# A new priority table for the first part of an attention and softplus-FFN kernel, and one transpose for the last keys of two tiles

## The chip, the cores and the metric

The kernel runs on one core of a Trainium2 chip. TensorE (PE in the profile, with PEld for its weight loads), VectorE (DVE), ScalarE (ACT), GpSimd (POOL) and SyncE (SP, which issues all the DMAs of this kernel) run side by side, each through its own instructions in their order, and wait for one another through semaphores. The metric is the device time of one execution in microseconds, as the median of several executions. Smaller is better.

## The reference

Keys and values are averaged over groups of 8 positions, attention runs over the 72 pooled positions, and the result goes through a two-layer network with softplus between.

```python
batch, n_heads, seq, head_dim = (8, 8, 576, 64)     # q, k, v
k_p = k.reshape(B, H, Sp, pool, D).mean(axis=3)      # pool = 8, Sp = 72
v_p = v.reshape(B, H, Sp, pool, D).mean(axis=3)
scores = scale * np.matmul(q, k_p.transpose(0, 1, 3, 2))
scores = scores - np.max(scores, axis=-1, keepdims=True)
attn = np.exp(scores)
attn = attn / (np.sum(attn, axis=-1, keepdims=True) + 1e-09)
attn_out = np.matmul(attn, v_p)
x = attn_out.transpose(0, 2, 1, 3).reshape(B * S, H * D)     # 4608 x 512
h = x @ w_in                                                 # 512 x 2048
g = np.maximum(h, 0.0) + np.log1p(np.exp(-np.abs(h)))
out = g @ w_out                                              # 2048 x 512
```

## The kernel before

The 4608 tokens are cut into 18 chunks of 256, each of two tiles of 128 tokens. A chunk goes through attention (`qTp`: transposes of q; `sc`: scores; `E`: exponentials; `pm` and `pe`: probabilities; `ptp` and `ltp`: their transposes; `avp`: products with the pooled values; `x`: the result, split into a high and a low part) and then through the network (`h`: first product; `g`: softplus; `acc` or `m`: second product). The network has 16 blocks f of 128 hidden units. Every product with a weight is made of three: high by high, low by high, high by low. So each block of w_in and w_out has to be rearranged and split first: SP loads it (`stage` for blocks 0 to 10, `wst` for blocks 11 to 15), DVE makes five passes over it (`bits`, `clamp`, `shift`, `sign`, `lowest`), ACT rounds it (`high`) and DVE subtracts (`rest`). The fourth pass (`sign`) of blocks 11 to 15 waits for block 10, since their results lie where `stage` was.

Of the 72 pooled keys of a head the first 64 are called main (`pm`, transposed in `PT` as `ptp`) and the last 8 are called the ends (`pe`, transposed as `ltp`). In `av_products` the ends need three copies of their probabilities in the partitions of `lt_`: high, low and high again, R = 32 rows each, for two halves of the heads.

The program has two parts. The first holds the pooling of batches 0 and 1 (`batch`), the conversion of all weight blocks (`weights`), the attention of chunks 0 to 3 (`attend`) and the network of chunks 0 to 2 (`feed`). The second part, from chunk 3 on, repeats one pattern until the end. In each part all operations are first written down as objects with an engine, a cost in microseconds, what they come after and the slots (PSUM banks, buffers) that they hold; `Order.run` then makes a schedule of them, engine by engine. Among operations that could start, it takes the one with the highest `rank` (the longest path of costs behind it) plus `first`. The table `HASTE` adds a number to `first` of single operations by their place in the list, for the first part alone. So costs and table set the order in which each engine, SP's queue included, gets its instructions, and which of several buffers they take. At run time each engine keeps to this order, and waits where something isn't there yet.

The names for what follows: `kvl` holds the last 64 positions of k and v of a batch, `kvst` half of its other keys or values, `kvlp` and `kps` are their pooling products on PE, `vps` the one for values, `kT` the transposed pooled keys. The exponentials of chunks 0 to 2 are made head by head from PSUM (`exp_sum`), those of chunk 3 at once (`exponential`); both need a table on ACT other than softplus does.

Of the kernel before, what the change touches and what calls it, by code (L numbers as in the profile page):

```python
# [9 lines left out]
F32 = mybir.dt.float32  # L10
# [98 lines left out]
def pooled_attention_softplus_ffn(  # L109
# [269 lines left out]
    class Tile:  # L379
# [47 lines left out]
        def exp_sum(self, j, ps, tag):  # L427
            if j == 0:
                self.sm = small.tile([P, H], F32, tag="sm" + tag, name="sm")
            for m in range(HP):  # L430
                h = 4 * (m // 2) + 2 * j + m % 2
                nc.scalar.activation(out=e_[self.c][:, self.t, h], in_=self.view(ps)[:, m],  # L432
                                     func=AF.Exp, scale=-1.0, bias=self.mn[:, j, m:m + 1],
                                     accum_out=self.sm[:, h:h + 1])
# [37 lines left out]
        def PT_out(self, ps):  # L472
            if self.c not in pt_:
                pt_[self.c] = one.tile([P, HP, CT], F32, tag="Z", name="pT")
            nc.scalar.copy(out=pt_[self.c][:, :, self.ts],
                           in_=ps.rearrange("p (m i) -> p m i", m=HP))

        def last(self, ps):
            for a in range(2):
                nc.tensor.transpose(out=ps[0:3 * R, a * P:(a + 1) * P],  # L480
                                    in_=self.pe[:, a].rearrange("p n k -> p (n k)"), identity=ident)

        def last_high(self, ps):

            if self.c not in last_:
                last_[self.c] = one.tile([3 * R, 2, CT], F32R, tag="Y", name="lt_")
            nc.scalar.copy(out=last_[self.c][:, :, self.ts],
                           in_=ps[0:3 * R, 0:2 * P].rearrange("p (a i) -> p a i", a=2))

        def last_low(self, ps):  # L490
            o = last_[self.c][R:2 * R, :, self.ts]
            nc.vector.tensor_tensor(
                out=o, in0=ps[R:2 * R, 0:2 * P].rearrange("p (a i) -> p a i", a=2),
                in1=o.bitcast(F32), op=ALU.subtract)

# [375 lines left out]
    def act(n):  # L871
        return 0.14 + 0.00094 * n
# [10 lines left out]
    def weights(f):  # L883
# [5 lines left out]
        def load(i):  # L889
            def fn():  # L890
                if early:
                    if not i:
                        x["raw"] = stage_at(f % NS)
                    st = x["raw"][:, 1 - i]
                else:
                    st = x["raw", i] = one.tile([P, 4 * 2 * P], I32, tag=stages[i].name, name="wst")
                if i:
                    nc.sync.dma_start(out=st, in_=wo32[f * P:(f + 1) * P, :])
                else:
                    for r in range(2):  # L900
# [85 lines left out]
    def batch(b):  # L986
# [23 lines left out]
        o_left = op(SYNC, 1.3, load_left, slots=[ld], lag=2.2)  # L1010
        o_k = [op(SYNC, 1.5, load(k, i), slots=[st[i]], lag=2.2) for i in range(2)]
        o_v = [op(SYNC, 1.5, load(v, i), slots=[vt[i] or vt[0]], lag=2.2) for i in range(2)]

# [21 lines left out]

        o = op(PE, 1.0, left_products, [o_left], [ld, s_left])
        o_kl = op(DVE, dve2(512), left_keys, [o], [s_left, s_kp])
# [7 lines left out]
        for i in range(2):  # L1045
# [10 lines left out]
            def products(i=i, N=N):  # L1056
                ps = bank(s_k, "kps").rearrange("p (h d) -> p h d", h=H)
                for r in range(N):
                    nc.tensor.matmul(out=ps[0:KM, HP * i:HP * (i + 1)], lhsT=zm,  # L1059
                                     rhs=x["k", i][:, :, r], start=r == 0, stop=r == N - 1)  # L1060
            halves.append(op(PE, 0.1 + 0.28 * N, products, [o, *halves], [st[i], s_k]))
# [4 lines left out]
        o = op(PE, 0.45, lambda: k_transposes(bank(s_t, "kT"), x["kp"]), [o, o_kl], [s_kp, s_t])  # L1066
        k_done[b] = [op(ACT, act(288), lambda: k_scaled(b, s_t.tile), [o], [s_t])]
# [18 lines left out]
    qT_done, score_done, av_done, k_ready, v_ready, made = {}, {}, {}, {}, {}, {}  # L1086

    def attend(c):
        s_lt, s_pT = Slot("lt_"), Slot("pT")
# [3 lines left out]
        for t in range(T):  # L1093
            def load(t=t):
# [10 lines left out]
        norms = []  # L1105
        for t, x in enumerate(tiles):
            keys = [o for b in sorted({b for _, _, b in spans(x.first, x.first + P)})
                    for o in k_done[b]]
            s_q, s_qT, s_E = Slot("bank"), Slot("qT"), Slot(f"E{t}")
            s_mn, s_sm, s_pm, s_pe = Slot("mn"), Slot("sm"), Slot("pm"), Slot("pe")  # L1110
            s_E = [s_E] if c < N1 else []
            o = op(PE, 0.5, lambda x=x, s=s_q: x.qT(bank(s, "qTp")),
                   [o_q[t], *([av[c - 1]] if c == N1 else [])], [s_q, *([s_q1] if c == 1 else [])])
# [30 lines left out]
        for x, ends, s_E, s_sm, s_pm, s_pe in norms:
# [4 lines left out]
            s, r = Slot("bank"), Slot("bank")  # L1149
# [141 lines left out]
    for i, x in HASTE.items():  # L1291
# [274 lines left out]
```

## Time and profile before

| what | value |
| --- | --- |
| time, median of 3 (range) | 885.15 us (884.62 to 886.55) |
| the profiled execution | 884.83 us, of which the span of instructions is 883.1 us |
| PE, DVE, ACT busy | 870.6, 645.2, 417.7 us |
| mean granted TensorE clock | 0.994 |

Times in the rows are microseconds from the start of the span unless ns stands beside them. "Busy" means that an instruction was in the engine; matmuls overlap, so that a row's duration can be longer than the distance to the next row's start, which is what the matmul costs in a stream. A timeline row gives start, duration, engine, line, operation, what it writes and reads, and in brackets how long the engine was idle before it and what ended that. The profile counts a product of plain fp32 data (a transpose not) as two instructions.

### The profile page before, as it was taken

Reading aid. Unit: us, or ns where it says so; the run is one execution under the profiler, and the core shown is the slowest. Engines: PE = TensorE matmul, PEld = TensorE weight load, DVE = VectorE, ACT = ScalarE, POOL = GpSimd, SP = SyncE. Lnnn points to the kernel's source line nnn. Section 1 sums busy time; section 2 is a strip of 40 time slices with the busy share of each in tenths; the row PEclk is TensorE's granted clock in tenths of the full one; section 3 lists DMA queues with packets and bytes.
Section 4 is the critical chain, followed back from the end, with each engine's and each line's share of the span. In section 5 each row is a group of like instructions: output and inputs, shape, how many; then the busy total and the mean of one; then the engine's idle time right before and its main releaser. Section 6 shows DMA issues by size and latency. Waiting matters only on the chain.

```text
span 883.1 us, 20500 instructions
## 1 busy us (share of the span) xinstructions
PE 870.6 (99%) x8280; PEld 827.1 (94%) x8280; DVE 645.2 (73%) x1601; ACT 417.7 (47%) x852; POOL 3.8 (0%) x33
## 2 busy tenths in 40 slices
PE   7999999999999999999999999999999999999997
PEld 3789989898899999999999999999999999999997
DVE  5899998878866868787767766778666565747454
ACT  4964333445445544544544445353545354444432
POOL 1000000000000000000000000000000000000000
PEclk7999999999999999999999999999999999999999
DMA  8975535455889768588757775678556556546472
GB/s 255 292 242 171 205 136 183 160 171 166 285 274 230 265 211 279 196 273 240 245 192 260 244 239 192 223 243 261 194 200 223 182 215 209 216 161 225 169 248 83
DMA packets 107086, 191.12 MB, mean 216 GB/s; under 512 B 46064, under 2 KB 60400, under 8 KB 106992
## 3 DMA queue, kind: packets, MB, share of 16 engines
q1 hardware_dynamic: 106992, 189.82, 64.6%
q8 instruction: 65, 1.06, 0.5%
q14 instruction: 29, 0.24, 0.1%
HBM read 167.25 MB, written 22.54 MB: 215 GB/s over the span
## 4 chain that ended last, share of the span: by engine, by line
PE 96%; DVE 1%; DMA 1%; ACT 1%; SPq 0%; issue 0%; DVEq 0%; ACTq 0%
PE h L675 37%; PE m L824 30%; PE acc L649 8%; PE h L627 7%; PE acc L716 3%; PE avp L594 2%; PE qTp L387 2%; PE ptp L468 2%; PE avp L601 2%; PE sc L515 1%; PE kps L1059 1%; DMA kvl<-in_v_dram 1%; DMA kvst<-in_k_dram 1%; ACT E L432 0%; PE m L515 0%; PE ltp L568 0%
## 5 line engine op out<-in xcount | busy, mean ns | idle before, releaser
L675 PE MATMUL h<-x,l 128*128 128x256 f32 x2748 | 335.0, 278 | 0.0
L675 PEld LDWEIGHTS h<-x,l 128*128 128x128 f32 x2748 | 321.1, 188 | 1.1
L683 ACT ACTIVATE g<-h 128x512 f32<-128x512 f32 x120 | 71.8, 598 | 261.7 <-PE h L675 261.5
L824 PE MATMUL m<-w,so 128*128 128x256 f32 x1134 | 147.1, 276 | 0.0
L824 PEld LDWEIGHTS m<-w,so 128*128 128x128 f32 x1134 | 137.1, 188 | 0.1
L734 DVE TENSOR_TENSOR sf<-g 128x128 f32<-128x128 f32 x112 | 32.7, 292 | 132.9 <-ACT g L683 132.9
L748 ACT CAST so<-sf 128x512 fp32r<-128x512 f32 x112 | 69.7, 622 | 69.5 <-DVE sf L737 68.7
L824 PE MATMUL m<-w,gh 128*128 128x256 f32 x476 | 91.2, 280 | 0.0
L753 DVE TENSOR_TENSOR so<-sf,so 128x512 fp32r<-128x512 f32 x112 | 77.3, 690 | 18.2 <-ACT so L748 16.5
L824 PEld LDWEIGHTS m<-w,gh 128*128 128x128 f32 x476 | 71.7, 188 | 0.0
L704 DVE TENSOR_TENSOR gl<-g,gh 128x384 fp32r<-128x384 f32 (+1 forms) x120 | 67.3, 561 | 2.4 <-ACT gh L697 2.4
L824 PE MATMUL m<-w,gl 128*128 128x256 f32 x238 | 65.8, 277 | 0.0
L697 ACT ACTIVATE gh<-h 128x384 fp32r<-128x384 f32 (+1 forms) x120 | 59.3, 494 | 0.0
L632 ACT ACTIVATE g<-h 128x256 fp32r<-128x256 f32 x96 | 32.0, 382 | 55.6 <-PE h L627 33.4
L627 PEld LDWEIGHTS h<-x,w 128*128 128x128 f32 x396 | 48.5, 188 | 2.7 <-ACT g L632 0.6
L627 PE MATMUL h<-x,w 128*128 128x256 f32 x396 | 49.8, 278 | 0.2 <-ACT g L632 0.2
L824 PEld LDWEIGHTS m<-w,gl 128*128 128x128 f32 x238 | 44.7, 188 | 0.0
L845 DVE TENSOR_TENSOR o<-o,m 128x256 f32<-128x256 f32 x98 | 39.8, 418 | 3.3 <-ACT o L837 0.4
L649 PE MATMUL acc<-w,g 128*128 128x512 f32 x132 | 41.9, 399 | 0.0
L824 PE MATMUL m<-l,gh 128*128 128x256 f32 x196 | 37.0, 277 | 0.0
L737 DVE TENSOR_TENSOR sf<-g,sf 128x128 f32<-128x128 f32 x112 | 32.7, 292 | 3.9
L438 DVE TENSOR_REDUCE sm<-E 128x8 f32<-128x576 f32 x30 | 21.2, 748 | 15.1 <-ACT E L350 15.1
(210 smaller groups left out, 1263.0 us busy)
## 6 DMA issues: line engine op xcount, KB each, us to landing
l<-wi SPq DMA_DIRECT2D x224, 512.0 KB
out_dram<-o SPq DMA_DIRECT2D x36, 256.0 KB
q<-in_q_dram SPq DMA_DIRECT2D x32, 256.0 KB
kst<-in_k_dram SPq DMA_DIRECT2D x24, 288.0 KB
vst<-in_v_dram SPq DMA_DIRECT2D x24, 256.0 KB
stage<-in_moe_w_in_dram SPq DMA_DIRECT2D x22, 256.0 KB
stage<-in_moe_w_out_dram SPq DMA_DIRECT2D x11, 512.0 KB
wi<-w SPq DMA_DIRECT2D x11, 512.0 KB
```

The lines of the kernel that those rows point to most:

```text
L627: nc.tensor.matmul(out=ps[:, 0:CT], lhsT=row(w, kc), rhs=x[:, kc], start=first and kc == j == 0, stop=last and kc == KC - 1 and j == 2)
L649: nc.tensor.matmul(out=accs[c][t], lhsT=a[:, ts], rhs=w, start=f == 0 and j == 0, stop=f == FC - 1 and j == 2)
L675: nc.tensor.matmul(out=ps[:, k * CT:(k + 1) * CT], lhsT=row(w, kc), rhs=x_[c][i][:, kc], start=first and n == 0, stop=last and n == len(or ...
L683: nc.scalar.activation(out=g, in_=x.rearrange("p (b i) -> p b i", i=P), func=AF.Softplus)
L697: nc.scalar.activation(out=gh, in_=quarters(c, x.rearrange("p (b i) -> p b i", i=P)), func=AF.Softplus)
L704: nc.vector.tensor_tensor(out=gl, in0=quarters(c, g), in1=gh.bitcast(F32), op=ALU.subtract)
L734: tt(out=sf[:, 2], in0=g[:, 0], in1=g[:, 2], op=ALU.add)
L737: tt(out=sf[:, 3], in0=g[:, 3], in1=sf[:, 1], op=ALU.subtract)
L748: nc.scalar.copy(out=so[:, 0], in_=ss[c, u])
L753: nc.vector.tensor_tensor(out=so[:, 1], in0=sf, in1=so[:, 0].bitcast(F32), op=ALU.subtract)
L824: nc.tensor.matmul(out=ms[c][n], lhsT=x, rhs=y, start=u == 0 and j == 0 and n in (1, 6, 5, 4), stop=u == FP - 1 and j == 2 and n in (2, 7, ...
L845: nc.vector.tensor_tensor(out=o, in0=in0, in1=m[n], op=how)
```

## The change

The rows and columns of the computation stay as they are. Four things differ:

1. `HASTE` holds other numbers, 587 in place of 110.
2. The costs of some operations are set otherwise: loads of k, v and weights 1.45 in place of 1.5, loads of q 1.0 in place of 1.4, and longer costs for the first PE operations (q transposes of chunk 0, pooling of batch 0).
3. The ends of both tiles of a chunk go into one tile `pe` of 64 columns a tile, with one DVE instruction a tile; two transposes a chunk (`pair_last`, 64 columns each) replace four (`last`, 96 columns each, with the three copies as columns). The three copies are now made when the result leaves PSUM: four ACT copies (`pair_high`) and two DVE subtractions (`pair_low_ends`) a chunk, in place of two and two, as the second part did already.
4. `AT_ONCE` is empty; what hangs on it isn't used.

```diff
@@ def exp_sum @@
-            if j == 0:
+            if not hasattr(self, "sm"):
...
-        def ends(self):
-            self.pe = one.tile([P, 2, 3, R], F32, tag="pe", name="pe")
-            for a in range(2):
-                hs = slice(4 * a, 4 * a + 4)
-                nc.vector.tensor_tensor(
-                    out=self.pe[:, a].rearrange("p n (h j) -> p n h j", h=4),
-                    in0=e_[self.c][:, self.t, hs, KM:SP].unsqueeze(1).to_broadcast([P, 3, 4, KL]),
-                    in1=self.sm[:, hs].unsqueeze(1).unsqueeze(3).to_broadcast([P, 3, 4, KL]),
-                    op=ALU.mult)
...
-        def last(self, ps):
-            for a in range(2):
-                nc.tensor.transpose(out=ps[0:3 * R, a * P:(a + 1) * P],
-                                    in_=self.pe[:, a].rearrange("p n k -> p (n k)"), identity=ident)
...
@@ def weights, batch, attend @@
-            return op(SYNC, 1.5, fn, slots=[stages[0 if early else i]], lag=2.2)
+            return op(SYNC, 1.45, fn, slots=[stages[0 if early else i]], lag=2.2)
...
-            o_q.append(op(SYNC, 1.4, load,
+            o_q.append(op(SYNC, 1.0, load,
...
-            o = op(DVE, 1.45, x.norm, ends, [*s_E, s_sm, s_pm, s_pe])
+            def norm(x=x):
+                x.reciprocal()
+                x.main()
+                pair_ends(c, x, "")
+            o = op(DVE, 1.27, norm, ends, [*s_E, s_sm, s_pm, s_pe])
...
-            p = op(PE, 0.3, lambda x=x, r=r: x.last(bank(r, "ltp")), [o], [r, s_pe])
-            h = op(ACT, act(256), lambda x=x, r=r: x.last_high(r.tile), [p], [r, s_lt])
-            lows.append(op(DVE, dve2(256), lambda x=x, r=r: x.last_low(r.tile), [h], [r, s_lt]))
+        s_l = Slot("bank")
+        p = op(PE, 0.25, lambda: pair_last(c, bank(s_l, "ltp")), e_c, [s_l, s_pe])
+        for a in range(2):
+            h = op(ACT, act(256), lambda a=a: pair_high(c, a, s_l.tile, a), [p], [s_l, s_lt])
+            lows.append(op(DVE, dve2(256), lambda a=a: pair_low_ends(c, a, s_l.tile), [h], [s_l, s_lt]))
+        for a in range(2):
+            lows.append(op(ACT, act(256), lambda a=a: pair_high(c, a, s_l.tile, 2), [p], [s_l, s_lt]))
...
-    HASTE = {27: -130, 29: -3, 34: -120, 36: -120, 45: 40, 46: 20, 48: -180, 55: -2, 56: -10,
...
+    HASTE = {-2: -1817.3, -1: -1988, 0: 3818, 1: 3695.9, 2: 2863.8, 3: 718.4, 4: 686.5, 5: -27.6, 6:
...
```

What this moves is seen in the order of the instructions. First the queue of SP at the program's start, before the change (`kvst_154` and `kvst_156` are the keys of batch 0, `kvl_158` its last positions, `q_162` the q of chunk 0 and later of chunk 2, `q_258` that of chunk 1, `kvst_247` and `kvst_327` the keys of batch 1):

```order
L1005 DMA kvst_154<-in_k_dram 128x4x256
L1005 DMA kvst_156<-in_k_dram 128x4x256
L994 DMA kvl_158<-in_k_dram 64x8x64
L994 DMA kvl_158<-in_v_dram 64x8x64
L358 DMA q_162<-in_q_dram 128x8x64 x2
L901 DMA stage_107<-in_moe_w_in_dram 128x2x256 x2
L898 DMA stage_107<-in_moe_w_out_dram 128x1024
L358 DMA q_162<-in_q_dram 128x8x64
L1005 DMA kvst_247<-in_k_dram 128x4x256
L358 DMA q_258<-in_q_dram 128x8x64 x2
L1005 DMA stage_107<-in_v_dram 128x4x256 x2
L1005 DMA kvst_327<-in_k_dram 128x4x256
```

And the same place after it (`kvl_163` belongs to batch 1, `q_177` to chunk 1, `wst_167` and `wst_188` to weight block 11, `q_263` to chunk 0; behind these come the loads of block 1 and of batch 0's values, mixed, then chunk 2's q and, mixed with block 2, the keys of batch 1):

```order
L961 DMA kvl_154<-in_k_dram 64x8x64
L961 DMA kvl_154<-in_v_dram 64x8x64
L972 DMA kvst_157<-in_k_dram 128x4x256
L972 DMA kvst_159<-in_k_dram 128x4x256
L961 DMA kvl_163<-in_k_dram 64x8x64
L961 DMA kvl_163<-in_v_dram 64x8x64
L868 DMA wst_167<-in_moe_w_in_dram 128x2x256 x2
L358 DMA q_177<-in_q_dram 128x8x64 x2
L865 DMA wst_188<-in_moe_w_out_dram 128x1024
L868 DMA stage_107<-in_moe_w_in_dram 128x2x256 x2
L865 DMA stage_107<-in_moe_w_out_dram 128x1024
L358 DMA q_263<-in_q_dram 128x8x64 x2
```

The last positions of both batches and the whole of block 11 move ahead; chunk 1 goes before chunk 0; the keys of batch 1 move back behind the values of batch 0 and two weight blocks.

Second, PE from its first product of the input on, before:

```order
L1059 MATMUL kps<-kvst,zm 64x256
L1018 MATMUL kvlp<-kvl,zl 72x512
L1059 MATMUL kps<-kvst,zm 64x256
L387 MATMUL qTp<-ident,q 128x128 x4
L259 MATMUL kT<-ident,kp 128x72 x4
L387 MATMUL qTp<-ident,q 128x128 x4
L407 MATMUL sc<-kT_98,qT 64x72 x32
L387 MATMUL qTp<-ident,q 128x128 x4
L1059 MATMUL kps<-kvst,zm 64x256 x4
L387 MATMUL qTp<-ident,q 128x128 x8
L407 MATMUL sc<-kT_98,qT 64x72 x16
L480 MATMUL ltp<-ident,pe 96x128 x2
```

And after, from the row behind the first scores (`sc ... x32`) on:

```order
L387 MATMUL qTp<-ident,q 128x128 x8
L407 MATMUL sc<-kT_98,qT 64x72 x16
L453 MATMUL ptp<-ident,pm 128x128 x4
L407 MATMUL sc<-kT_98,qT 64x72 x16
L453 MATMUL ptp<-ident,pm 128x128 x4
L535 MATMUL ltp<-ident,pe 64x128 x2
L1044 MATMUL vps<-stage,zm 64x128 x16
L387 MATMUL qTp<-ident,q 128x128 x4
L1026 MATMUL kps<-kvst,zm 64x256 x4
L561 MATMUL avp<-pT,vs_101 64x256 x8
L568 MATMUL avp<-lt__392,vlo_103 128x256 x4
L453 MATMUL ptp<-ident,pm 128x128 x4
```

Ahead of these rows PE has `kvlp`, `kps`, `kvlp`, `kps` and then the same four rows from `qTp` to `sc` as before. The pooling of batch 1's keys (`kps` of four matmuls) has moved from ahead of the second chunk's attention to behind `vps`. Behind these rows come its second half, the last transposes of q of chunk 2, `ptp`, `ltp`, `kT`, the scores of chunk 2, `vps` of batch 1 and the first `h`.

Third, PE at the attention of chunk 3. Before, its scores stood among the first blocks of the network, some 80 rows into PE's list:

```order
L407 MATMUL sc<-kT_100,qT 64x72 x16
L627 MATMUL h<-x,w 128x256 x24
L407 MATMUL sc<-kT_100,qT 64x72 x16
L649 MATMUL acc<-w,g 128x512 x2
L649 MATMUL acc<-w,gl 128x512
```

After, those of its second tile stand near the end of the first part, some 260 rows into the list, and all that hangs on them comes behind:

```order
L407 MATMUL sc<-kT_100,qT 64x72 x16
L594 MATMUL h<-x,l 128x256 x24
L616 MATMUL acc<-l,g 128x512 x2
L616 MATMUL acc<-l,gl 128x512
L616 MATMUL acc<-l,g 128x512 x2
L616 MATMUL acc<-l,gl 128x512
L616 MATMUL acc<-l,g 128x512 x2
L616 MATMUL acc<-l,gl 128x512
L616 MATMUL acc<-l,g 128x512 x2
L616 MATMUL acc<-l,gl 128x512
L594 MATMUL h<-x,l 128x256 x24
L453 MATMUL ptp<-ident,pm 128x128 x4
```

So the exponentials of chunk 3, with their two loads of ACT's table, move from the start of the network to its last block. From the second part's first products on, PE has the same rows in the same order, but for one group of `qTp` and `sc` that stands a place later.

More of the change, by code (lines that the diff above doesn't have):

```diff
@@ L891, in fn @@
                 if early:
-                    if not i:
+                    if "raw" not in x:
                         x["raw"] = stage_at(f % NS)
@@ L1010, in batch @@
         o_left = op(SYNC, 1.3, load_left, slots=[ld], lag=2.2)
-        o_k = [op(SYNC, 1.5, load(k, i), slots=[st[i]], lag=2.2) for i in range(2)]
-        o_v = [op(SYNC, 1.5, load(v, i), slots=[vt[i] or vt[0]], lag=2.2) for i in range(2)]
+        o_k = [op(SYNC, 1.45, load(k, i), slots=[st[i]], lag=2.2) for i in range(2)]
+        o_v = [op(SYNC, 1.45, load(v, i), slots=[vt[i] or vt[0]], lag=2.2) for i in range(2)]
         s_left, s_kp, s_vp = Slot("bank"), Slot("kp"), Slot("vp")
@@ L1034, in left_values @@
                 in1=lmask.unsqueeze(1).unsqueeze(3).to_broadcast([R, 2, 4, D]), op=ALU.mult)
-        o = op(PE, 1.0, left_products, [o_left], [ld, s_left])
+        o = op(PE, 1.0 if b else 1.4, left_products, [o_left], [ld, s_left])
         o_kl = op(DVE, dve2(512), left_keys, [o], [s_left, s_kp])
@@ L1060, in products @@
                                      rhs=x["k", i][:, :, r], start=r == 0, stop=r == N - 1)
-            halves.append(op(PE, 0.1 + 0.28 * N, products, [o, *halves], [st[i], s_k]))
+            halves.append(op(PE, 0.1 + 0.28 * N + (0.4 if b == 0 and i else 0), products, [o, *halves], [st[i], s_k]))
         o = op(ACT, act(512), lambda: nc.scalar.copy(
@@ L1065, in batch @@
         s_t = Slot("bank")
-        o = op(PE, 0.45, lambda: k_transposes(bank(s_t, "kT"), x["kp"]), [o, o_kl], [s_kp, s_t])
+        o = op(PE, 0.45 if b else 0.7, lambda: k_transposes(bank(s_t, "kT"), x["kp"]), [o, o_kl],
+               [s_kp, s_t])
         k_done[b] = [op(ACT, act(288), lambda: k_scaled(b, s_t.tile), [o], [s_t])]
@@ L1086, in pooled_attention_softplus_ffn @@
     qT_done, score_done, av_done, k_ready, v_ready, made = {}, {}, {}, {}, {}, {}
+    AT_ONCE = ()
     def attend(c):
@@ L1109, in attend @@
             s_q, s_qT, s_E = Slot("bank"), Slot("qT"), Slot(f"E{t}")
-            s_mn, s_sm, s_pm, s_pe = Slot("mn"), Slot("sm"), Slot("pm"), Slot("pe")
+            s_mn, s_sm, s_pm = Slot("mn"), Slot("sm"), Slot("pm")
             s_E = [s_E] if c < N1 else []
-            o = op(PE, 0.5, lambda x=x, s=s_q: x.qT(bank(s, "qTp")),
+            o = op(PE, 0.5 if c else (1.1, 0.75)[t], lambda x=x, s=s_q: x.qT(bank(s, "qTp")),
                    [o_q[t], *([av[c - 1]] if c == N1 else [])], [s_q, *([s_q1] if c == 1 else [])])
@@ L1122, in attend @@
                        [s, s_mn])
-                if c < N1:
+                if c < N1 and c not in AT_ONCE:
                     def exp_sum(x=x, i=i, s=s, e=s_E[0], t=t, n=s_sm):
-                        if c == 0 and 0 not in e_:
+                        if 0 not in e_:
                             new_E(0)
@@ L1132, in less @@
                     def less(x=x, i=i, s=s):
-                        if c not in e_:
+                        if c in AT_ONCE:
+                            if 0 not in e_:
+                                new_E(0)
+                            e_[c] = e_[0]
+                        elif c not in e_:
                             new_E(c)
                         x.less(i, s.tile)
-                    ends.append(op(DVE, 0.46, less, [d, *e_free], [s, s_mn]))
-            if c < N1:
+                    ends.append(op(DVE, 0.46, less, [d, *(e_free if c == N1 else ())], [s, s_mn, *s_E]))
+            if c in AT_ONCE:
+                o = op(ACT, 0.68, lambda x=x: exponential(e_[c][:, x.t]), ends, s_E, table="exp")
+                exps.append(o)
+                ends = [op(DVE, 0.76, lambda x=x, n=s_sm: x.sum(n.name), [o], [s_sm, *s_E])]
+            elif c < N1:
                 exps.extend(ends)
@@ L1140, in attend @@
                 subs += ends
-            norms.append((x, ends, s_E, s_sm, s_pm, s_pe))
+            norms.append((x, ends, s_E, s_sm, s_pm))
         if c == N1:
             ex = op(ACT, 1.2, lambda: exponential(e_[c]), subs, table="exp")
-        for x, ends, s_E, s_sm, s_pm, s_pe in norms:
+        for x, ends, s_E, s_sm, s_pm in norms:
             if c == N1:
                 ends = [op(DVE, 0.75, lambda x=x, n=s_sm: x.sum(n.name), [ex], [s_sm])]
-            o = op(DVE, 1.45, x.norm, ends, [*s_E, s_sm, s_pm, s_pe])
+            def norm(x=x):
[3 more added lines that the diff above has]
+            o = op(DVE, 1.27, norm, ends, [*s_E, s_sm, s_pm, s_pe])
             e_c.append(o)
-            s, r = Slot("bank"), Slot("bank")
+            s = Slot("bank")
             p = op(PE, 0.5, lambda x=x, s=s: x.PT(bank(s, "ptp")), [o], [s, s_pm])
             lows.append(op(ACT, act(512), lambda x=x, s=s: x.PT_out(s.tile), [p], [s, s_pT]))
-            p = op(PE, 0.3, lambda x=x, r=r: x.last(bank(r, "ltp")), [o], [r, s_pe])
-            h = op(ACT, act(256), lambda x=x, r=r: x.last_high(r.tile), [p], [r, s_lt])
-            lows.append(op(DVE, dve2(256), lambda x=x, r=r: x.last_low(r.tile), [h], [r, s_lt]))
+        s_l = Slot("bank")
[5 more added lines that the diff above has]
+            lows.append(op(ACT, act(256), lambda a=a: pair_high(c, a, s_l.tile, 2), [p], [s_l, s_lt]))
         e_free[:] = e_c
```

16 lines of the change are left out of this document (1 added, 15 removed), and 91 rows, old and new, of the table HASTE.

## The prediction

> **What bounds the kernel now.** First the page: its span, the busy times and the chain that ended last.
>
> ```profile
> span 883.1 us, 20500 instructions
> PE 870.6 (99%) x8280; PEld 827.1 (94%) x8280; DVE 645.2 (73%) x1601; ACT 417.7 (47%) x852; POOL 3.8 (0%) x33
> PE 96%; DVE 1%; DMA 1%; ACT 1%; SPq 0%; issue 0%; DVEq 0%; ACTq 0%
> ```
>
> PE is the bound nearly everywhere: 883.1 - 870.6 = 12.5 us of the span are without it. The table by stretches (length, then busy time and count of PE, PEld, DVE, ACT, POOL, then granted clock, DMA share, GB/s) tells where they lie; I cut the start at the steps of the clock.
>
> ```profile
> 4.70:8.12 3.42, 1.46 (x5) 0.40 (x4) 2.14 (x4) 0.00 (x0) 0.00 (x0) 1.00 1.22 303
> 8.12:11.53 3.41, 3.41 (x14) 2.11 (x14) 1.37 (x2) 1.27 (x3) 0.00 (x0) 0.50 0.87 300
> 11.53:14.94 3.41, 1.76 (x67) 1.30 (x65) 2.05 (x5) 3.15 (x16) 0.00 (x0) 1.00 0.52 124
> 14.94:18.36 3.42, 2.50 (x8) 1.57 (x9) 3.35 (x5) 3.40 (x22) 0.00 (x0) 0.50 1.10 294
> 18.36:21.77 3.41, 3.41 (x12) 2.07 (x11) 2.49 (x7) 0.94 (x3) 0.00 (x0) 0.50 1.05 355
> 21.77:25.18 3.41, 3.24 (x81) 2.61 (x81) 1.90 (x7) 3.32 (x8) 0.00 (x0) 1.00 1.04 264
> 32.00:40.00 8.00, 7.42 (x125) 6.09 (x118) 7.75 (x16) 6.88 (x32) 0.00 (x0) 1.00 1.04 306
> 40.00:45.50 5.50, 4.86 (x45) 3.64 (x45) 4.81 (x14) 5.42 (x19) 0.00 (x0) 1.00 1.07 397
> 45.50:183.87 138.37, 137.94 (x995) 122.76 (x994) 127.91 (x230) 60.82 (x139) 0.00 (x0) 1.00 0.53 177
> ```
>
> From 45.5 us to the second part's first product (at some 183.7) PE lacks 0.43 us. DVE is at 127.9 of 138.4 there and yet starves nobody. From 32 to 45.5 PE lacks 0.58 + 0.64 = 1.22 us. All else that a new order can win lies in the first 25 us, where the list of PE's waits names the loads:
>
> ```profile
> PE qTp L387 <- DMA q<-in_q_dram: 1.7, 1, 1.7
> PE kps L1059 <- DVE kvst L1052: 1.0, 1, 1.0
> PE kvlp L1018 <- DMA kvl<-in_v_dram: 1.0, 1, 1.0
> PE kps L1059 <- DMA kvst<-in_k_dram: 0.9, 1, 0.9
> ```
>
> The second part keeps its rows on PE, and I count it unchanged. So the question is when PE has done the first part's work.
>
> **The last keys.** The timeline has a pair of `ltp` and what follows it; the answer on the tile `ltp` has both widths (ns, min/median/max).
>
> ```profile
> 27.05 0.42 PE L480 MATMUL ltp<-ident,pe 128*96 128x128 f32 x2
> 27.31 0.60 PE L468 MATMUL ptp<-ident,pm 128*128 128x128 f32 x4
> ...
> L568 PE MATMUL ltp<-ident,pe x28: 271/272/272, 219.5 to 822.9; 128*64 128x128 f32 x28
> L480 PE MATMUL ltp<-ident,pe x16: 271/273/315, 23.0 to 71.9; 128*96 128x128 f32 x16
> L487 ACT CAST lt__372<-ltp x2: 368/370/371, 24.4 to 27.5; 96x256 fp32r<-96x256 f32 x2
> ```
>
> A pair holds PE for 27.31 - 27.05 = 0.26 us, and 64 columns take as long as 96. Eight pairs become four: 4 x 0.26 = **1.0 us less on PE**, half of it before 45 us. ACT gets 16 copies in place of 8, at 47% busy; DVE loses eight products. Between `ltp` and the `avp` that waits for those copies the new order has `vps`, `qTp` and `kps` (over 5 us) for chunk 1; I cost them at nothing. Without that cover the four copies would show, some 1.5 us at 0.37 us each.
>
> **The queue of loads.** Rates first: around 7 us q moves, around 20 us k and v, around 53 us blocks with long rows.
>
> ```profile
> 6.00:8.00 2.00, 1.05 (x4) 0.23 (x3) 1.12 (x2) 0.00 (x0) 0.00 (x0) 1.00 1.27 286
> 19.00:22.00 3.00, 3.00 (x12) 1.91 (x10) 1.88 (x5) 0.56 (x2) 0.00 (x0) 0.54 1.07 362
> 52.00:54.00 2.00, 2.00 (x39) 1.38 (x37) 1.97 (x3) 1.24 (x3) 0.00 (x0) 1.00 0.96 379
> ...
> 7.34 0.47 SPq L898 DMA_DIRECT2D stage<-in_moe_w_out_dram  x1
> 11.94 0.37 SPq L358 DMA_DIRECT2D q<-in_q_dram  x1
> ...
> 7.43 1.28 PE L1018 MATMUL kvlp<-kvl,zl 128*72 128x512 f32 x2 [0.95 <-DMA kvl<-in_v_dram]
> ```
>
> So 0.52 MB of k, v or w_in take 0.52/362 GB/s = 1.45 us, of w_out 1.38, a tile of q or a `kvl` (0.26 MB) 0.92. Before, 1.31 MB had landed at 7.4; they take 2.90 + 0.92 us, so a load lands at about 3.5 us plus the sum of the queue up to it. Before, SP stood still from 7.8 to 11.9 on a q whose buffer PE still read (124 GB/s in that stretch); the new order has no such wait there, but 1 MB of block 11 stands ahead (2.8 us). Its landings: `kvl` 4.4, keys 5.9 and 7.3, second `kvl` 8.2, block 11's w_in 9.7, chunk 1's q 10.6 and 11.5, w_out 12.9, block 0 15.7, chunk 0's q 16.6 and 17.6, block 1 and the values of batch 0 mixed until 23.3, chunk 2's q 25.2, keys of batch 1 26.6 and 29.4.
>
> **PE along the new order**, with these rows' durations (the 37.77 and 74.98 rows are from the chain of waits: the exponentials of eight heads, and two `h`; the last is a group, with its mean in ns):
>
> ```profile
> 8.64 1.11 PE L1059 MATMUL kps<-kvst,zm 128*64 128x256 f32 x2
> 9.69 1.12 PE L387 MATMUL qTp<-ident,q 128*128 128x128 f32 x4
> 11.84 1.48 PE L407 MATMUL sc<-kT,qT 64*64 64x72 f32 x64
> 16.95 3.65 PE L1059 MATMUL kps<-kvst,zm 128*64 128x256 f32 x8 [0.89 <-DMA kvst<-in_k_dram]
> 24.55 2.57 PE L1076 MATMUL vps<-stage,zm 128*64 128x128 f32 x32
> 27.84 1.94 PE L1059 MATMUL kps<-kvst,zm 128*64 128x256 f32 x8
> 31.16 1.09 PE L594 MATMUL avp<-pT,vs 64*64 64x256 f32 x16
> 45.50 0.71 PE L649 MATMUL acc<-w,g 128*128 128x512 f32 x2
> ...
> 37.77 2.54 ACT E L432 x16
> 74.98 2.73 PE h L627 x24
> ...
> L947 DVE SCALAR_TENSOR_TENSOR stage<-stage 128x1024 int32<-128x1024 int32 x11 | 13.4, 1222 | 0.2
> ```
>
> `kvlp`, `kps`, `kvlp`, `kps` are paced by loads and DVE's sums and end at 10.6; transposes and scores of chunk 1 end at 14.7 (before: 13.3 for chunk 0). PE then waits for q until 16.6, and the second chunk's transposes, scores, `ptp` and `ltp`, paced by ACT's exponentials of chunk 1 (5 us from 14 on), end at 22.2. `vps` waits for its second half until 23.3 and ends at 24.8, `qTp` at 25.5, the first four `kps` run from 26.6 to 28.5, `avp` (1.09 + 0.73) to 30.3, `ptp` and the other `kps` (no wait: 29.4 is past) to 32.8, `qTp`, `ptp`, `ltp`, `kT` to 34.8, then 0.5 us until ACT has scaled kT, chunk 2's scores to 37.0, `vps` to 39.6. The first `h` needs chunk 1's low part: in DVE's list two conversion passes of 1.22 us and three reductions stand ahead of its second half, which I find done at 40.7. `h` ends at 41.8, `avp` 43.6, `h` 45.0, `ptp` 45.5, and the first `acc` starts at **45.5, as before**.
>
> The work behind that point differs. The new order has one `h` more done, half of 2.73 = 1.37 us; it has one `ptp` (27.84 - 27.31 = 0.53) and chunk 2's `ltp` (0.26) still ahead, and 0.2 less for chunk 3's: -1.37 + 0.53 + 0.26 - 0.2 = **-0.8 us**. Of before's 0.43 us of idle behind 45.5 I take 0.42 as gone, and **+0.3** for new small waits (bounds: 0, and 1.2 as in the 13.5 us before).
>
> **Chunk 3 at the end.** ACT's rows for its exponentials:
>
> ```profile
> 59.09 1.28 ACT L350 ACT_TABLE_LOAD   x1
> 60.38 1.17 ACT L350 ACTIVATE E<-E 128x1152 f32<-128x1152 f32 x1
> ```
>
> Two loads and the exponentials keep softplus off ACT for 1.28 + 1.17 + 1.28 = 3.7 us. Behind the scores PE has two `h` and two `acc`, 5.5 us, and the next `h` needs one bank that softplus empties first: hidden, cost nothing; with the cover gone up to 3.7 us. The early passes over block 11 cost DVE idle time alone.
>
> **Sum:** -0.8 - 0.4 + 0.3 = -0.9 us, 884.83 - 0.9 = 883.9 against the profiled execution; that one lies 0.32 below the median, so 884.2.
>
> **A rule against it.** The table's clock column: after 8.12 to 11.53 and 18.36 to 21.77, with PE busy throughout, the clock is 1.00; after 2.50 of 3.42 us it is still 0.50. At 0.50 four `kps` took 3.65 us, at 1.00 1.94. In the new order the stretch from 18.4 to 21.8 is busy for some 2.4 us only. The Trainium skill, TensorE: Matmul & The Clock Gate, section "Part 1: The HAM clock gate", says that a sustained busy window releases the clock and an idle one of 3.4 us takes it back, which these rows bear out; its Part 4 adds that transposes don't count as busy the same way, though here the window from 8.12 held eight q and four key transposes and was followed by 1.00. By that rule the new start would warm up later, which is the second rival.
>
> **Rivals.** (1) Faster: the loads come earlier than my sums and DVE's tail at 40.7 shrinks, so that all idle after 32 us goes: 1.22 + 0.43 + 1.0 for the keys, and 0.6 at the start: -3.2, 881.9. For it: 397 GB/s at 40 to 45.5. Against: q moves at 286. (2) Slower: the clock stays at 0.50 until 28.6. `vps` costs 2.57 x 0.88 = 2.3 more, two `kps` 3.4, `avp` 0.9; 1.8 us of waits for loads absorb some: +4.8 - 1.9 (what else is gained) = +2.9, 888.0. It decides if PE isn't busy through one whole window before `vps` ends; `vps` itself, at 0.50, would fill the window until 25.2, which speaks against it. (3) A load behind the wrong one: batch 1's last values are issued behind chunk 3's q, which waits until PE has read chunk 2's (33.2); I find them landed at 37.4 and needed at 38.2. Two microseconds later they cost 1.2: 885.4. (4) The new numbers do nothing on the chip: 885.1.
>
> **Chances.** Forecast 0.45, rival 1 0.30, rival 2 0.10, 3 and 4 together 0.15. The forecast's own range, 882.9 to 885.8, follows from 0 to 1.2 for new waits and about 1 us of error in the landings. A difference of 0.2% (1.8 us) is about what a measurement of this kernel can tell from no change. Faster than 883.4: 0.33; within: 0.51; slower than 886.9: 0.16, with half of it for covers that fail at the end. The range reaches from rival 1 to short of rival 2: 881.8 to 886.8.
>
> **What would show it.** PE idle ahead of chunk 0's `qTp` near 16.6 and of batch 1's `kps` near 26.6; clock 1.00 from 25.2 at the latest; the first `acc` at 45.5 +- 1; eight L535 transposes in the first part; no idle on PE behind chunk 3's scores. I am wrong if the first `acc` comes before 44 or after 47, or if PE loses over 1 us behind it.

## The result, and the profile after

The changed kernel took 894.32 us (median of 5 runs, 892.54 to 896.6), the kernel before 884.67 us beside it (median of 5): ratio 1.0103, 95% interval 1.0082 to 1.0125. It is some 9 us slower; the forecast was 884.2 us, and the range ended at 886.8. The profiled execution is the slowest of the five, 896.6 us.

From the page of the changed kernel: the span, the busy times and the shares of the chain of waits.

```profile
span 894.9 us, 20493 instructions
...
PE 873.4 (98%) x8272; PEld 828.9 (93%) x8272; DVE 643.4 (72%) x1593; ACT 421.0 (47%) x860; POOL 3.8 (0%) x33
...
PE 95%; DMA 2%; SPq 1%; DVE 1%; issue 0%; ACT 0%; DVEq 0%; ACTq 0%
```

PE is without work for 894.9 - 873.4 = 21.5 us, 9.0 more than before, and the chain has 2% of DMA and 1% of SP's sequencer. The list of PE's waits says where:

```profile
PE qTp L387 <- DMA q<-in_q_dram: 4.1, 1, 4.1
PE vps L1044 <- DMA kvst<-in_v_dram: 3.6, 1, 3.6
PE vps L1044 <- DMA stage<-in_v_dram: 2.2, 1, 2.2
PE kps L1026 <- DVE kvst L1019: 2.0, 1, 2.0
```

All four lie ahead of the first `acc`. PE's timeline up to it (start, length, tile, and in brackets the idle time before it with its releaser):

```profile
9.64 1.11 PE L1026 MATMUL kps<-kvst,zm 128*64 128x256 f32 x2 [2.02 <-DVE kvst L1019]
...
21.36 2.04 PE L387 MATMUL qTp<-ident,q 128*128 128x128 f32 x8 [4.12 <-DMA q<-in_q_dram]
...
30.79 2.46 PE L1044 MATMUL vps<-stage,zm 128*64 128x128 f32 x16 [2.17 <-DMA stage<-in_v_dram]
...
42.58 1.23 PE L407 MATMUL sc<-kT,qT 64*64 64x72 f32 x64 [0.69 <-ACT kT L265]
47.38 4.61 PE L1044 MATMUL vps<-kvst,zm 128*64 128x128 f32 x32 [3.57 <-DMA kvst<-in_v_dram]
...
56.82 0.71 PE L616 MATMUL acc<-w,g 128*128 128x512 f32 x2
```

The first `acc` starts at 56.82 in place of 45.50: 11.3 us, nearly all of the 11.8 us between the two spans. Behind it the table by stretches and the waits from 60 us on have next to nothing:

```profile
56.82:194.50 137.68, 136.88 (x981) 121.40 (x979) 121.46 (x220) 61.06 (x142) 0.00 (x0) 1.00 0.48 160
...
180.00:200.00 20.00, 20.00 (x142) 17.30 (x142) 13.49 (x34) 12.31 (x27) 0.00 (x0) 1.00 0.10 37
```

```profile
PE acc L616 <- DVE gl L605: 0.8, 2, 0.4
```

Why the loads are late stands in SP's own timeline. SP issues every load, in the order of the program (the second number is the time that the issue took):

```profile
4.11 0.64 SPq L961 DMA_DIRECT2D kvl<-in_v_dram  x1
7.65 0.89 SPq L868 DMA_DIRECT2D wst<-in_moe_w_in_dram  x2
10.79 0.99 SPq L358 DMA_DIRECT2D q<-in_q_dram  x2
12.77 0.34 SPq L865 DMA_DIRECT2D wst<-in_moe_w_out_dram  x1
...
25.81 4.72 SPq L972 DMA_DIRECT2D kvst<-in_k_dram  x1
...
36.42 0.37 SPq L972 DMA_DIRECT2D kvst<-in_v_dram  x1
41.02 0.37 SPq L358 DMA_DIRECT2D q<-in_q_dram  x1
41.44 0.57 SPq L972 DMA_DIRECT2D kvst<-in_v_dram  x1
```

And the list of SP's waits names the readers at three of the stops:

```profile
SPq L358 <- PE qTp L387: 4.1, 1, 4.1
SPq L358 <- PE kps L1026: 2.2, 1, 2.2
SPq L868 <- PE kvlp L985: 2.1, 1, 2.1
```

Between 4.75 and 12.77 us SP stands three times, each time on a load whose buffer PE still reads: w_in of block 11 waits for the first `kvlp`, chunk 1's q for the first `kps`, w_out of block 12 for the second `kvlp`. (Ahead of the prediction that w_out, `wst_188`, is put down to block 11; it is block 12's, of the same size.) Chunk 0's q, which has a buffer of its own, is issued behind them at 14.65. Between 36.8 and 41.0 SP stands on chunk 3's q, with the last half of batch 1's values behind it. The transfers dry up at both places, and at a third between them (length, PE, PEld, DVE, ACT, POOL, clock, DMA share, GB/s):

```profile
8.00:12.00 4.00, 2.33 (x4) 0.60 (x4) 3.46 (x7) 1.24 (x2) 0.00 (x0) 1.00 0.54 161
...
28.00:32.00 4.00, 1.83 (x20) 1.59 (x17) 2.55 (x5) 3.39 (x19) 0.00 (x0) 0.91 0.73 161
...
40.00:44.00 4.00, 3.12 (x80) 2.50 (x78) 2.61 (x3) 3.36 (x8) 0.00 (x0) 1.00 0.55 145
44.00:48.00 4.00, 0.62 (x3) 0.65 (x4) 3.77 (x7) 3.55 (x19) 0.00 (x0) 0.62 1.03 336
```

The third place is the row at 25.81: SP took 4.72 us for one issue, that of batch 1's first keys. What held it the trace doesn't tell. Batch 0's last values, for which PE waits 2.17 us at 30.79, had been issued ahead of it, at 21.81. In seven of the kernels below (in the table, from `keys_first` to `late_q3_keys_q0`) the same issue takes 3.95 to 4.27 us, and none of them tests it.

So theory **H**: loads that wait for a buffer, or for a reader, stop SP with every load behind them. Its rivals: **S**, the first transfer (`kvl`, pieces of 256 bytes) is slow and holds the start; **C**, the clock is at 0.50 for longer; **rival 3** of the prediction, the one q alone; **K**, the edit of the last keys itself costs time.

### The profile page after: what moved, and what is told of

Same layout as the page of the kernel before. It is cut to its first block, busy times and chain, and to the rows that moved or that the text cites. A ratio compares the mean times of both kernels' runs of the same rounds, so it can differ in the third digit from the quotient of the medians.

```text
span 894.9 us, 20493 instructions
## 1 busy us (share of the span) xinstructions
PE 873.4 (98%) x8272; PEld 828.9 (93%) x8272; DVE 643.4 (72%) x1593; ACT 421.0 (47%) x860; POOL 3.8 (0%) x33
## 4 chain that ended last, share of the span: by engine, by line
PE 95%; DMA 2%; SPq 1%; DVE 1%; issue 0%; ACT 0%; DVEq 0%; ACTq 0%
PE h L642 37%; PE m L791 30%; PE h L594 7%; PE acc L616 7%; PE acc L683 3%; PE avp L561 2%; PE qTp L387 2%; PE ptp L453 2%; PE avp L568 2%; PE sc L482 1%; DMA stage<-in_v_dram 1%; PE vps L1044 1%; DMA kvst<-in_k_dram 1%; DMA kvst<-in_v_dram 1%; SPq L868 1%; PE kps L1026 1%
```

## The experiments

Ratios are to the kernel before, run in between on the same chip; its median was between 884.1 and 884.9 us each time. "First acc" is read from one profiled execution, and scatters: the changed kernel and `q3_behind` have the same instructions in the same order until 36 us, and yet their `avp` of chunk 1 starts at 36.32 in one and at 34.86 in the other. The changed kernel's 56.8 comes from an execution 2.3 us above its median.

| kernel | median us | ratio, 95% interval | first acc us |
| --- | --- | --- | --- |
| changed kernel | 894.3 | 1.0103 (1.0082 to 1.0125) | 56.8 |
| keys_first | 894.2 | 1.0105 (1.0081 to 1.0129) | 55.0 |
| late_away | 893.3 | 1.0099 (1.0085 to 1.0113) | 54.0 |
| q3_behind | 891.2 | 1.0079 (1.0061 to 1.0097) | 51.5 |
| fill_v | 892.4 | 1.0094 (1.0071 to 1.0116) | 53.0 |
| late_q3 | 889.6 | 1.0053 (1.0035 to 1.0071) | 48.5 |
| late_q3_keys | 887.7 | 1.0030 (1.0019 to 1.0041) | 47.6 |
| late_q3_keys_q0 | 887.9 | 1.0030 (1.0019 to 1.0042) | 47.6 |
| low_behind | 887.3 | 1.0030 (1.0019 to 1.0041) | 47.5 |
| late_q3_keys_qT | 887.8 | 1.0034 (1.0021 to 1.0048) | 48.5 |
| late_q3_keys_pool | 887.2 | 1.0026 (1.0014 to 1.0038) | 48.7 |
| block2_later | 890.3 | 1.0060 (1.0042 to 1.0078) | 45.9 |
| block2_low | 889.7 | 1.0052 (1.0035 to 1.0070) | 46.6 |
| keys_alone | 885.6 | 1.0015 (1.0003 to 1.0028) | 46.9 |
| keys_alone_copies | 887.2 | 1.0029 (1.0011 to 1.0046) | 47.1 |
| keys_alone_pool | 884.4 | 1.0000 (0.9988 to 1.0011) | 43.4 |
| keys_pool_low | 885.7 | 1.0004 (0.9991 to 1.0017) | 46.1 |

Most edits move single operations in the order that the planner returned: `behind(i, j)` puts operation i (numbered as in `HASTE`) right behind j, `ahead(i, j)` right ahead of it.

### One load, or one pair of loads, at a time

```diff
 order = todo.run()
+for i in (11, 12, 13):             # keys_first
+    ahead(i, 5)
+behind(0, 1)
```

> The changed kernel, with the first two loads of keys ahead of the load of the last rows, and the first product of the keys ahead of that of the last rows, as in the kernel before. Theory S (the start is slow because the transfer with pieces of 256 bytes goes first): the first keys land near 4.6 us instead of 8.4, PE's first kps starts near 6, chunk 1's q is issued near 7 instead of 10.8, and the first acc comes 3 to 4 us earlier, at 53 to 54; total 890 to 892. Theory H (later loads wait for buffers that two blocks of weights hold, so the start isn't what sets the end): the first acc comes less than 2 us earlier; total 893 to 895.

```diff
+number(25).slots[0].name, number(26).slots[0].name = "X6", "L"     # late_away
+for i in (168, 150):
+    behind(i, 218)
+for i in (154, 153, 152):
+    behind(i, 148)
+for i in (178, 177, 176):
+    behind(i, 156)
```

> The changed kernel, with w_in of block 11 and w_out of block 12 loaded (and their six first passes on DVE made) later, behind the other loads of late blocks; the two load buffers that they held take batch 1's values. Theory H: the stop of SP from 4.75 to 7.65 and the one to 12.77 are gone, 1.05 MB less stands ahead of chunk 0's q and of the values, and batch 1's values no longer wait for the products of its keys; its last half is issued right behind chunk 3's q. First acc 4 to 6 us earlier, at 51 to 53; total 888 to 891. Theories S and C (slow first transfer; cold clock): under 2 us of gain, 893 to 895.

```diff
+behind(505, 25)                    # q3_behind
```

> The changed kernel, with the load of chunk 3's first half of q issued behind the last half of batch 1's values. Rival 3 of the prediction (the q of chunk 3, which waits until PE has read chunk 2's, holds the values up): the wait of vps for them, 3.57 us, goes nearly whole, first acc at 53 to 54, total 891. Theory H: the values' buffer is that of the second keys, whose product ends at about 40.4, so they are issued only 1 us earlier than at 41.44; first acc 0.5 to 1.2 us earlier, total 893 to 894.

No theory hit all three. `keys_first` came as H said, and `late_away` lies at 893.3, where S and C had it: alone the two gain nothing that the intervals show, though the first `acc` came 1.8 and 2.8 us earlier. `q3_behind` came at rival 3's 891, some 2 to 3 us lower and more than H allowed; likely rather than certain, since its interval and that of the changed kernel overlap. Its SP and PE rows:

```profile
34.96 4.37 SPq L972 DMA_DIRECT2D kvst<-in_v_dram  x2
39.55 0.99 SPq L358 DMA_DIRECT2D q<-in_q_dram  x2
...
42.88 2.54 PE L1044 MATMUL vps<-kvst,zm 128*64 128x128 f32 x32 [0.53 <-DMA kvst<-in_v_dram]
```

The last half is issued by 39.33, as soon as the second `kps` has left its buffer, and `vps` starts 3.6 us later; in the changed kernel 5.4 us passed between the end of its issue (42.0) and `vps`, with q ahead of it and a queue that had run dry. `vps` then takes 2.54 us in place of 4.61: the shorter wait keeps the clock.

In `late_away` the same half had a free buffer, yet was issued at 38.38, behind the q. Each edit leaves the other's stop in place. That calls for both. Nor did `late_away` take away the stop at the start, as H had expected it to: SP stood from 4.75 to 10.28 on chunk 1's q, whose buffer the first `kps` reads, and the transfers fell to 62 GB/s from 8 to 12 us.

```diff
 def value_products():
+    for n in range(14 if b else 0):                                # fill_v
+        nc.tensor.matmul(out=bank(s_v, "vps")[:, 0:P], lhsT=ident, rhs=ident, start=True, stop=True)
     ps = bank(s_v, "vps")...
```

> The changed kernel with 14 products of 128 by 128 on PE ahead of batch 1's value products, where PE waits 3.57 us for their load (their results are overwritten). Theory C (the clock, let go in that wait, costs part of the loss): the value products run at full clock, 2.5 us instead of 4.6, and the first h 1.4 instead of 1.6; first acc 2 us earlier, total 892. Rival (the clock isn't the loss, and the products come too early or run into the landing): no gain, total 894 to 895.

PE's rows there:

```profile
42.27 3.39 PE L1041 MATMUL vps<-ident 128*128 128x128 f32 x28
45.59 2.57 PE L1046 MATMUL vps<-kvst,zm 128*64 128x128 f32 x32
```

With PE kept busy through the wait the value products take 2.57 us, as C said. The total is 892.4 against 894.3, but the intervals overlap: C is a term of about 2 us at this place (4.61 less 2.57 on PE), and a consequence of the wait for the load.

### Loads together

`late_q3` makes the edits of `late_away` and `q3_behind`, `late_q3_keys` those of `keys_first` too, and `late_q3_keys_q0` adds

```diff
+for i in (235, 236):
+    ahead(i, 269)
```

> The changed kernel with both: the loads of blocks 11 and 12 later (their buffers taken by batch 1's values), and chunk 3's q behind those values. Theory H (two stops of SP, one by buffers at the start, one by q at 37 to 41): both values are issued near 32 and land by 37, so the wait of vps goes whole and vps takes 2.5 us instead of 4.7; first acc at 48 to 49.5, total 886.5 to 888.5. Rival (both edits remove the same wait, and what is left is the start): first acc at 51 to 52, total 890.

> As late_q3, and the first two loads of keys ahead of the load of the last rows. Theory S (the slow first transfer holds the start): 2 to 3 us less than late_q3, first acc at 46 to 47, total 884.5 to 886. Theory H (the start goes by chunk 1's q, which waits for the buffer of the first keys in either order): less than 1 us from late_q3.

> As late_q3_keys, and chunk 0's q, which has a buffer of its own, loaded ahead of chunk 1's. Theory H (SP stands still until the first keys' product is done, with loads behind it that need no such wait): the queue is fed from 5 us on, PE's wait before chunk 0's transposes (1.8 to 4.1 us) goes, first acc 1.5 to 3 us earlier than late_q3_keys, total at or under the kernel before (883 to 885). Rival (the DMA engines are full by then, so the order only shifts the wait to chunk 1's q): no gain over late_q3_keys.

`late_q3`, SP and PE:

```profile
30.22 0.98 SPq L972 DMA_DIRECT2D kvst<-in_v_dram  x2
...
39.31 2.54 PE L1044 MATMUL vps<-kvst,zm 128*64 128x128 f32 x32
...
48.49 0.71 PE L616 MATMUL acc<-w,g 128*128 128x512 f32 x2
```

Both halves go out at 30.2, and the wait of `vps` is gone. Half of the loss is given back (ratio 1.0053 against 1.0103, intervals clear of each other), 1 us less than expected. The stop at the start stays, from 4.75 to 8.89 us, again on chunk 1's q. The keys' order, worth nothing alone, then gives about 2 us more (1.0030; the intervals just touch): the gain that S expected, though not its total, and the stop ends at 6.98. Chunk 0's q ahead of chunk 1's gives nothing: the four issues of both took SP 6.00 us (from 4.72 to 10.72), though the buffer was free at 7.1. Something other than the buffer held them, which fits the rival; the DMA share was 0.93 from 4.7 to 10.7.

### The last keys

`keys_alone` is the kernel before, operation by operation in its old order and buffers, with only the last keys as in the change.

> The kernel before in its old order, with the last keys transposed once for both tiles and nothing else. Theory H (the loss lies in the order of the loads, the edit of the last keys is harmless): four pairs of transposes of 0.26 us go from PE, half of them before the first acc; first acc at 45.0 to 45.6, total 0.5 to 1.0 us below the kernel before. Rival K (the four copies of 32 rows and the later start of the first tile's part hold avp up): first acc 1.5 us later or more, total 1 to 4 us above the kernel before.

It is slower, not faster, as K said (1.0015, 1.0003 to 1.0028). ACT's groups between 20 and 46 us (busy time, mean ns of one), before and in `keys_alone`:

```profile
L487 ACT CAST lt__372<-ltp 96x256 fp32r<-96x256 f32 x2 | 0.7, 370 | 0.0
```

```profile
L541 ACT CAST lt__411<-ltp 32x256 fp32r<-32x256 f32 x4 | 1.4, 362 | 0.0
```

A copy of 32 rows takes as long as one of 96, so a pair costs ACT 1.4 us in place of 0.7. ACT idles there for 3.9 us in 26, nearly all of it waiting for PE; from 36 to 44 us it is busy for 7.89 of 8 us (7.93 before). And PE now waits for its exponentials, which empty the bank that `vps` needs:

```profile
38.87 2.57 PE L1044 MATMUL vps<-kvst,zm 128*64 128x128 f32 x32 [1.04 <-ACT E L432]
```

Two more kernels tell the place of the copies from their time:

```diff
+for i in (297, 296, 294, 292):     # keys_alone_copies
+    behind(i, 316)
```

> As keys_alone (the kernel before with the last keys alone changed), with ACT's four copies of chunk 1's last keys behind two of chunk 2's four groups of exponentials instead of ahead of them. Theory K (the copies, 1.5 us of ACT, hold up the exponentials that free the bank of batch 1's vps): its wait of 1.04 us goes, first acc at 45.6 to 46.2, total 0.7 to 1.2 us below keys_alone, 0.2 to 0.8 above the kernel before. Rival (keys_alone differs from the kernel before by scatter of the loads): total as keys_alone, 1.5 above the kernel before.

```diff
 def pair_high(c, a, ps, row):
+    if row == 2 and c <= N1:       # keys_alone_pool, late_q3_keys_pool
+        nc.gpsimd.tensor_copy(out=last_[c][2 * R:3 * R, a], in_=last_[c][a * R:(a + 1) * R, a])
+        return
```

> As keys_alone, with the second two of ACT's four copies of the last keys (rows 64 to 96) made by GpSimd out of the first two, in the first part's four pairs. Theory K (keys_alone is 1.5 us above the kernel before because ACT, full there, makes four copies of 0.37 us a pair where it made two): ACT has as much to do as before, first acc at 45.0 to 46.0, total 0.7 to 1.5 us below keys_alone, at the kernel before or up to 0.5 us under it. Rival (the price is the later start: both tiles' last keys wait for the second tile): total as keys_alone, 1.5 above the kernel before.

Moved on ACT the copies gain nothing: the wait of `vps` goes, but chunk 1's `ptp` then waits 1.8 us for ACT, and 887.2 is above what either side had. Taken off ACT they do: 884.4, level with the kernel before, and the wait of `vps` falls from 1.04 to 0.41 us. The intervals of `keys_alone` and `keys_alone_pool` overlap a little, so the 1.2 us between them are likely rather than certain. The first `acc` at 43.4 is no measure of the copies: of the 3.5 us by which it lies ahead of `keys_alone`, 2.4 are there before any of them (`kps` at 15.47 and 17.82). And the 0.41 us that is left, with no such wait in the kernel before, fits the rival, by which the later start has a price of its own. A last step, to bring the transposes' gain home:

```diff
+for i in (293, 295):               # keys_pool_low
+    ahead(i, 29)
```

> As keys_alone_pool, and on DVE the two low parts of chunk 1's last keys placed ahead of the sums of batch 1's last rows, where DVE then waits 0.60 us for ACT. Theory K, taken further: avp's wait of 0.81 us for these parts falls to 0.2, total 0.5 to 0.7 us below keys_alone_pool and the kernel before, 883.7 to 884.0. Rival (the order of DVE only shifts a wait to chunk 2's probabilities): as keys_alone_pool, 884.4.

No gain (1.0004): the wait moved, as the rival said, to chunk 2's `ltp`, 1.4 us for `pe`. None of the kernels is shown to be faster than the kernel before.

### What is left in late_q3_keys

Four places in its trace, from PE's waits up to 60 us, PE's timeline and DVE's:

```profile
PE sc L407 <- ACT qT L394: 2.2, 1, 2.2
```

```profile
29.06 1.91 PE L1026 MATMUL kps<-kvst,zm 128*64 128x256 f32 x8 [1.12 <-DMA kvst<-in_k_dram]
...
42.89 1.42 PE L594 MATMUL h<-x,w 128*128 128x256 f32 x10 [1.24 <-DVE x L578]
```

```profile
38.75 0.42 DVE L545 TENSOR_TENSOR lt__508<-ltp,lt__508 32x256 fp32r<-32x256 f32 x1 [1.46 <-ACT lt__508 L541]
```

```diff
+behind(261, 300)                   # low_behind, block2_low
```

> As late_q3_keys, and on DVE one product of chunk 1's last keys (the low part of 32 rows) placed behind the two low parts of chunk 1's x that the first h reads. Theory K (DVE stands 1.46 us for ACT's four copies of the last keys, and the x that the first h waits 1.24 us for stands behind it): that wait goes, first acc at 46.2 to 46.8 instead of 47.6, total 1.0 to 1.4 us below late_q3_keys, 886.3 to 886.7. Rival (the low part is then late for chunk 1's avp, or DVE has the same work in another order): total as late_q3_keys, 887.7.

```diff
+for i in (61, 60):                 # block2_later, block2_low
+    behind(i, 25)
+for i in (62, 63, 64):
+    ahead(i, 65)
```

> As late_q3_keys, and the two loads of block 2 (1.05 MB, first of all weights in the changed order, needed only by the third h) moved behind batch 1's values, their three early passes on DVE ahead of block 2's fourth. Theory H (loads in the order of issue: what stands ahead in the queue delays batch 1's keys): these land about 2.5 us earlier, the wait of kps for them (1.12 us) goes, first acc at 46.3 to 46.8, total 886.3 to 887. Rival (the passes, 2.1 us on a DVE that is full there, make PE wait behind the first acc): total 888 to 889.

> Both edits, of low_behind and of block2_later. If both theories hold, their gains add: first acc at 45.0 to 45.8, total 885.0 to 885.8, about 1 us above the kernel before. If they remove the same wait, 886.5.

> As late_q3_keys, with the same copies on GpSimd. Theory K: DVE's stop of 1.46 us for those copies and the wait of the first h go, total 0.8 to 1.5 us below late_q3_keys, 886.2 to 886.9; what is then left over the kernel before, some 2 us, is the order of the chunks and blocks. Rival: 887.7 as before, and all of it is the order.

```diff
+behind(244, 236)                   # late_q3_keys_qT
+behind(237, 236)
+ahead(238, 277)
+ahead(245, 284)
```

> As late_q3_keys, with ACT's two copies of chunk 0's transposed q one group of exponentials of chunk 1 earlier. Theory A (with chunk 1 first, chunk 0's scores wait 2.17 us for ACT, and this sets the first acc): the wait falls to about 1 us, first acc 1 us earlier, total 886.7. Theory H (batch 1's keys, the next load needed, set it): the wait moves to kps, first acc within 0.4 us of late_q3_keys, total 887.7.

`low_behind` halves the wait of `h` (to 0.54 us) and stays within the interval of `late_q3_keys`. `late_q3_keys_qT` gains nothing, as H said: the wait of `sc` goes, but `ptp` then waits 1.3 us for `pm`, and `kps` still 1.1 us for its load. `late_q3_keys_pool` is 0.5 us lower, less than the intervals tell, and its `h` still waits 1.3 us. `block2_low` lies at 889.7: the gains of its two edits neither add up nor fall together. `block2_later` brings the first `acc` to 45.9, where it stood before, and is 2.6 us **slower** than `late_q3_keys`. PE's waits there name the reason, which the rival had (its 888 to 889 was too low):

```profile
PE acc L616 <- DVE gl L605: 2.0, 3, 1.3
PE h L594 <- DVE x L578: 1.1, 1, 1.1
PE h L594 <- DVE w L928: 0.8, 1, 0.8
```

The waits for `gl` and `w` lie behind the first `acc`, that for `x` ahead of it; `late_q3_keys` has 0.4 us for `gl` there and none for `w`. Three passes that DVE made between 16 and 21 us, where it had idle time, now stand in its full stretch, and are paid for behind the first `acc`. An early first `acc` is thus no gain by itself.

## Why the prediction was wrong

**The queue of loads** is the step that failed: "a load lands at about 3.5 us plus the sum of the queue up to it", and "Before, SP stood still from 7.8 to 11.9 on a q whose buffer PE still read [...]; the new order has no such wait there". It has three such waits in the first 13 us and a fourth at 37. I added up bytes in the order of issue and didn't ask of each load which buffer it takes and who reads that last, though the same kind of stop stood in the trace of before. In the changed order two of the four load buffers hold late blocks of weights from 7.65 us on, so that batch 1's keys and values share the other two. Forecast and measured: first `kps` pair done 10.6 and 13.7, chunk 0's first q used at 16.6 and 21.4, first `vps` done 24.8 and 33.2, second `vps` started 37.0 and 47.4. With the values' stops taken away (`late_q3`) 4.7 us come back, and with the keys first too (`late_q3_keys`) the first `acc` comes at 47.6, two above my 45.5, and 6 of the 9 us are gone. What the stops at the start cost by themselves isn't shown. The rates were too high as well: 286 to 379 GB/s were taken, and that kernel, with a queue never dry until 24 us, moved 253 to 314.

**Rival 3** was the right mechanism with the wrong price: 1.2 us, in 0.15 of the chances that it shared with rival 4. Alone it is likely worth some 2 to 3 us: `vps` waited 0.53 us in place of 3.57 and took 2.54 in place of 4.61. With the buffers freed too, the pair gives 4.7.

**Rival 2**, the clock: right in direction, and mostly a consequence of the waits. The windows of 0.50 add up to at least 13.7 us (the first step in the trace is at 14.24) against 10.2 before, and lie later. Of the 11.8 us between the spans 9.0 are waits; PE is busy 2.8 us longer though the last keys take about 1.0 from it, so that some 3.8 us, by estimate, are work at the lower clock. The dearest window follows the wait of 3.57 us:

```profile
41.55:44.96 3.41, 1.57 (x69) 1.28 (x67) 1.92 (x3) 2.98 (x8) 0.00 (x0) 1.00 0.83 225
...
44.96:51.78 6.82, 4.40 (x32) 4.31 (x32) 6.66 (x14) 6.59 (x34) 0.00 (x0) 0.50 0.98 336
```

`fill_v` puts its size there at about 2 us. By the Trainium skill, TensorE: Matmul & The Clock Gate, section "Part 1: The HAM clock gate", an idle window of 3.4 us takes the clock back. The trace agrees only in part: the window ahead of 44.96 wasn't idle, PE was busy in it for 1.57 us, and yet 0.50 followed; so it did behind 1.24 us of work (27.89 to 31.30) and, before the change, behind 1.76 (11.53 to 14.94), while 2.35 us (14.24 to 17.65) kept 1.00. So "which these rows bear out" in the prediction holds for the release alone. My condition for this rival (no window busy throughout before `vps` ends) was not the one that mattered; the waits were: `vps` took 2.5 us behind 0.5 us of waiting and 4.6 behind 3.6.

**The last keys** were sized from one side only. PE's 1.0 us is there in rows (two transposes of 0.27 us hold it for 0.26 a pair), but in the old order the edit made the kernel 1.3 us dearer where I had 1.0 us less. The likely reason is ACT's copies, which "I cost them at nothing" left out: 0.7 us a pair more, at a stretch in which ACT is full. The 47% of ACT that I quoted is a mean over the whole span. In the new order, of which I had said it, the cover seems to have held on PE: `avp` of chunk 1 starts without a wait at 36.32 and that of chunk 0 at 53.49, and GpSimd's copies gave only 0.5 us, within the intervals.

**Chunk 3 at the end** costs nothing, as forecast: PE is busy for 20.00 of 20 us from 180 on.

**Behind the first acc** I forecast 0.9 us less than before. The spans leave 894.9 - 56.8 = 838.1 us there against 883.1 - 45.5 = 837.6, with 0.8 us of waits against 0.3. The same stretch is 837.2 in `keys_first` and 838.6 in `q3_behind`, so that 0.8 us can't be told here; this stays open.

**Still open:** the last 2 to 3 us of `late_q3_keys`. The last keys may be a part (1.2 us in the old order, 0.5 us measured in the new). For the rest the trace names waits of 1 to 2 us on loads, on DVE and on ACT; those that were taken away came back elsewhere. Nor was the long issue of batch 1's first keys tested: in `late_q3_keys` it takes 4.27 us from 21.33 on, the transfers fall to 163 GB/s from 24 to 28, and `kps` waits 1.12 us for keys.

## What to carry to other kernels

Where one engine issues all loads in program order, price a new order load by load: which buffer it takes, who reads that buffer last and when, and what is queued behind it; a sum of bytes is only the lower bound. A load that must wait is worth trying behind those that needn't: for chunk 3's q this was likely worth 2 to 3 us, for chunk 1's q at the start nothing. Freeing one of two stops in a row may show little until both are gone. An engine's share of the whole span says nothing about a stretch in which it is full: the second 0.36 us copies there probably cost more than the transposes saved.

## What the runs showed of the hardware

A copy on ACT took 362 ns for 32 rows of 256 and 370 ns for 96. GpSimd, reading SBUF, took 0.84 to 0.85 us for two of 32 rows, and 1.67 once. The start differs from run to run: the first `kvlp` took 1.95 us in the changed kernel and 1.05 in `q3_behind`, with the same instructions ahead. The same section of the Trainium skill calls the window free-running, so that it falls differently in each run; the table's column shows 1.00 and 0.97 there, and only the durations tell the two apart (a `kvlp` that starts at 9.48 in `keys_first`, in a window of 0.50, takes 1.95 us too).
